# Symmetric sums of keys by VectorE's block turn instead of TensorE, with a new order of the kernel's work

## The chip, the cores and the metric

The kernel runs on one core of a Trainium2 chip. The metric is the device time of one execution in microseconds (us). The core has five engines with instruction queues of their own: TensorE (PE in the profile, its weight loads PEld), VectorE (DVE), ScalarE (ACT), GpSimd (POOL) and SyncE (SP, which here only starts DMAs). They meet through semaphores.

## What is computed

Four batches, four heads, 1088 positions, 32 values per head, in float32. First an attention whose features are products of two sketches of 8 numbers, then a mixing of tokens with phases and a channel step on its output:

```python
a, b = S1 x, S2 x                        # per position: 8 numbers each
phi(x) = a_i * b_j                       # 64 features
kv = sum_s phi(k)_f v_d ;  z = sum_s phi(k)_f
x  = (phi(q) kv) / (phi(q) z + 1e-6)     # attention, heads side by side: B, S, 128
theta = x @ w_theta
y  = w_tok_r @ (x cos theta) + w_tok_i @ (x sin theta)
u  = x + y
out = u + max(u @ w_ch, 0)
```

The denominator phi(q) z can be small, so the kernel computes it with more than float32's precision. It uses that z is S1 K S2 with K the sum of k k^T over positions, a symmetric 32x32 matrix for each head ("key sums"). Each k is split into a rounded part kb (16 bits) and a rest r; K is kb kb^T, exact, plus the rest's terms. With kh = k + kb the term r kh^T, halved and added to its own transpose, gives the rest of K.

## The kernel before

Every operation of the kernel is first recorded with its engine, its buffers and what it depends on, and gets a number. A tuple ORDER, made ahead of time by a planner, then says in which order all operations are issued; each engine works off its own operations in that order, one after another. A second tuple, SLOTS, gives each buffer its place in SBUF or PSUM, and an operation that takes a place over waits for the buffer that was there. So an instruction that waits holds up everything behind it on its engine, and the number of an operation in a list of its engine tells who stands behind whom.

The stages that matter here:

- **key sums** (`key_sums`), one for each batch: TensorE adds up kb kb^T and r kh^T into PSUM. ScalarE copies both out (`ksum`, the second halved). Then `corners`, on TensorE: for each head two matmuls of 32x32 with the identity add the halved rest and its transpose into a third place of the PSUM tile, from which ScalarE later copies it (`e2`).
- **chain** (`chain`), for batch 0, batch 1 and for batches 2 and 3 together: ScalarE rounds K to a level `e0`, VectorE subtracts (`e1`), and `first` multiplies e0, e1 and e2 by the sketch on TensorE. Some ten short steps follow that alternate between VectorE, ScalarE and TensorE and end in the factors of the denominator (`cut`), which the batch's "levels" need.
- **levels, den, num**: the attention's output xT of a batch, with columns of 1152 positions. The queries were rounded before (`q0`) and the rest subtracted by VectorE.
- **turn** (batches 1 to 3): xT is turned to positions by rows, VectorE in 32x32 blocks and then a write to HBM (`far`) and four reads back (`xk`), both issued by SyncE. VectorE multiplies xk by the cosines and sines of theta (`z`).
- **rows**: w_tok has 17 rows of 1088 columns and arrives as 64-bit words, loaded by SyncE into `raw` buffers (class `zs`, 5 places, which z, qt and xk also use). ScalarE makes two conversions of each (L576, L578) and VectorE two integer steps (L316, L312, the custom instruction).
- **mix**: matmuls of z with the rows, in full float32, for batch 0 with all columns of a row at once (three matmuls of 384, 384 and 320 columns), for batch 1 in three groups of columns; batches 2 and 3 together in a Winograd form of seven products. `out` adds x, multiplies by w_ch and stores.

TensorE's mixing matmuls also fill its time between other stages. L332 is the line of the helper for all matmuls, L312 that of tensor-tensor operations on VectorE and GpSimd, L316 and L319 those of other arithmetic; tiles tell them apart.

Of the kernel before, what the change touches and what calls it, by code (L numbers as in the profile page):

```python
# [102 lines left out]
XTURN = (1, 2, 3)  # L103
PARTS = ((0, 384), (384, 544))
# [141 lines left out]
def kernel(  # L246
# [363 lines left out]
    def key_sums(b):  # L610
# [64 lines left out]
        g = kg[b, 0] = buf("g1", (2 if KDMA[b] else 3, D), F32, "ksum")  # L675
        op("A", act(D), lambda: A.copy(g()[:, 0], t()[:, 0]), [(g, 0)], [(t, "s")])
        at("rest", b)
        if KDMA[b]:
            for c in range(NC):
                op("P", TILE32, lambda c=c: heads(1, rc()[:, c * HD:(c + 1) * HD], kh()[:, c]), [(t, "l")], [r, kh])  # L680
            op("A", act(D), lambda: A.mul(g()[:, 1], t()[:, 1], 0.5), [(g, 1)], [t])
            op("P", 0.3, lambda: corners(2, [(g()[:, 1], None), (None, g()[:, 1])]), [t], [(g, 1)])
        else:
            for c in range(NC):
                def two(c=c):
                    x = rc()[:, c * HD:(c + 1) * HD]
                    heads(1, x, kc()[:, c * HD:(c + 1) * HD])
# [791 lines left out]
```

## Time and profile before

| | us |
|---|---|
| median of 3 runs (lowest, highest) | 216.03 (215.62, 216.91) |
| the profiled execution: time | 215.9 |
| its span, first to last instruction | 214.1 |
| TensorE busy in it | 207.0 |
| VectorE busy | 180.7 |
| ScalarE busy | 113.4 |
| GpSimd busy | 37.2 |

The granted TensorE clock was 0.999 over the span. In a timeline row the first number is the start and the second the length in us, then engine, line, operation, tiles written and read, partitions and columns, and the count; in square brackets stands the engine's idle time before it and what ended it. A group row gives the sum in us and, behind the comma, the mean of one in ns. A row of stretches gives the length, then each engine's busy time and count, the clock, the share of the DMA engines and GB/s.

### The profile page before, as it was taken

How to read it: one execution, taken by the hardware profiler on the slowest of the kernel's cores; microseconds unless marked ns; L12 is line 12 of the kernel's file. 1: busy time of each engine (PE TensorE's matmuls, PEld its weight loads, DVE VectorE, ACT ScalarE, POOL GpSimd, SP SyncE). 2: the span in 40 equal slices, each digit the busy share in tenths (PEclk: the TensorE clock that was granted, in tenths of full speed). 3: DMA queues.
4: the chain of work that ended last, by engine and by line, in shares of the span. 5: the costliest groups of instructions: out<-in, count | busy, mean ns of one | idle time of the engine just before them, and what ended most of it. 6: DMA issues, size and time to landing. Idle time of an engine off the chain costs nothing.

```text
span 214.1 us, 5301 instructions
## 1 busy us (share of the span) xinstructions
PE 207.0 (97%) x2140; PEld 149.7 (70%) x2140; DVE 180.7 (84%) x359; ACT 113.4 (53%) x240; POOL 37.2 (17%) x87
## 2 busy tenths in 40 slices
PE   7899999999999999999999999999999999999992
PEld 7677798968867676775665776666676776676682
DVE  1799999999999998997999999988579599995232
ACT  4899999999998986697531333149700000000000
POOL 1272740306400000840003010000040020020002
PEclk9999999999999999999999999999999999999999
DMA  6999999996996994093000443120590011213503
GB/s 222 393 417 418 384 368 418 420 341 120 357 281 214 431 423 201 29 330 72 0 0 7 69 117 106 32 39 22 174 161 0 0 40 27 40 37 52 92 0 67
DMA packets 28780, 37.06 MB, mean 173 GB/s; under 512 B 21332, under 2 KB 23812, under 8 KB 26580
## 3 DMA queue, kind: packets, MB, share of 16 engines
q1 hardware_dynamic: 23268, 31.91, 42.7%
q0 software_dynamic: 1488, 3.15, 7.0%
q10 hardware_dynamic: 4000, 1.67, 3.0%
q8 instruction: 17, 0.28, 0.5%
q14 instruction: 7, 0.06, 0.1%
HBM read 29.84 MB, written 4.00 MB: 158 GB/s over the span
## 4 chain that ended last, share of the span: by engine, by line
PE 55%; DVE 18%; issue 11%; ACT 6%; DMA 6%; POOL 1%; SPq 1%; POOLq 0%; DVEq 0%; ACTq 0%
PE ps L332 49%; DVE big L312 7%; DMA zs<-far 3%; DMA st<-s 2%; PE ps L1053 2%; PE ps L951 2%; ACT big L626 2%; DVE big L319 1%; DMA far<-zs 1%; DVE g L312 1%; DVE zs L312 1%; DVE big L316 1%; ACT g L726 1%; PE ps L361 1%; POOL out L1236 1%
## 5 line engine op out<-in xcount | busy, mean ns | idle before, releaser
L332 PE MATMUL ps<-big,zs 128*128 128x384 f32 (+2 forms) x380 | 108.9, 435 | 0.3 <-DVE zs L312 0.3
L332 PEld LDWEIGHTS ps<-big,zs 128*128 128x128 f32 x380 | 67.1, 190 | 34.8 <-issue 0.9
L1277 ACT COPY g<-ps 80x256 f32<-80x256 f32 x1 | 0.4, 368 | 55.4 <-PE ps L1270 55.4
L332 PE MATMUL ps<-big,big 128*32 128x32 f32 (+2 forms) x352 | 21.8, 234 | 0.0
L312 DVE CUSTOM_DVE_ANT_0 big<-big,big 128x2176 uint16<-128x2176 uint16 x17 | 21.6, 1282 | 0.1
L578 ACT ACTIVATE big<-zs 128x1088 int32<-128x1088 uint32 (+1 forms) x18 | 21.4, 1193 | 0.4 <-DVE g L312 0.4
L576 ACT ACTIVATE big<-zs 128x1088 f32<-128x1088 f32 x17 | 20.8, 1225 | 0.7 <-DVE lv L312 0.5
L332 PEld LDWEIGHTS ps<-big,big 128*32 128x32 f32 (+1 forms) x352 | 14.9, 124 | 5.6 <-issue 1.0
L312 DVE TENSOR_TENSOR big<-big,big 128x544 f32<-128x544 f32 x24 | 16.7, 714 | 0.1
L326 POOL DMA_DIRECT2D g<-big x6 | 5.3, 1071 | 56.2 <-ACT g L1213 56.2
L312 DVE TENSOR_TENSOR zs<-zs,g 128x384 f32<-128x384 f32 (+2 forms) x24 | 9.9, 450 | 4.7 <-DMA zs<-far 4.7
L1236 POOL DMA_DIRECT2D out<-g x6 | 3.8, 633 | 49.7 <-DVE g L1240 31.8
L316 DVE TENSOR_SCALAR big<-big 128x1088 int32<-128x1088 int32 x17 | 12.3, 721 | 0.0
L361 PE MATMUL ps<-idle 128*128 128x112 bf16 (+1 forms) x67 | 10.0, 312 | 1.3 <-POOL idle L363 1.3
L312 DVE TENSOR_TENSOR g<-lv 128x768 f32<-128x768 f32 x12 | 11.2, 950 | 0.1
L312 DVE TENSOR_TENSOR big<-big,hf 128x1152 f32<-128x1152 f32 x8 | 10.7, 1351 | 0.0
L332 PE MATMUL ps<-mf,big 128*128 128x96 f32 (+1 forms) x72 | 10.0, 277 | 0.4 <-DVE big L312 0.4
L332 PE MATMUL ps<-sbk,g 128*128 128x64 f32 x72 | 10.0, 276 | 0.3 <-ACT g L726 0.3
L332 PE MATMUL ps<-w,big 128*128 128x128 f32 (+1 forms) x76 | 10.2, 278 | 0.0
L1139 ACT ACTIVATE g<-g 128x384 f32<-128x384 f32 x12 | 6.3, 531 | 6.9 <-DVE g L319 6.9
L332 PEld LDWEIGHTS ps<-w,big 128*128 128x128 f32 (+1 forms) x76 | 9.4, 189 | 0.5
L332 PEld LDWEIGHTS ps<-sbk,g 128*128 128x128 f32 x72 | 9.0, 191 | 0.8 <-ACT g L726 0.6
(198 smaller groups left out, 352.9 us busy)
## 6 DMA issues: line engine op xcount, KB each, us to landing
zs<-w_tok SPq DMA_DIRECT2D x17, 1088.0 KB, 10.6
big<-k_l SPq DMA_DIRECT2D x5, 576.0 KB, 12.5
big<-v_l SPq DMA_DIRECT2D x4, 576.0 KB, 15.5
big<-q_l SPq DMA_DIRECT2D x3, 576.0 KB, 10.4
big<-hf POOLq DMA_DIRECT2D x3, 576.0 KB, 10.1
far<-zs SPq DMA_DIRECT2D x3, 576.0 KB, 4.4
zs<-far SPq DMA_DIRECT2D x12, 144.0 KB, 4.2
big<-k_l ACTq DMA_DIRECT2D x2, 576.0 KB, 4.4
```

Of the source, the lines that this page charges most:

```text
L312: eng.tensor_tensor(out=o, in0=a, in1=b, op=f)
L316: (eng or V).tensor_scalar(out=o, in0=a, scalar1=s1, scalar2=s2, op0=op0, **kw)
L326: op("G", 0.9, lambda: G.dma_start(dst(), src(), accum_op=ALU.add), w, r, fly=fly)
L332: T.matmul(o, lhs, rhs, start=start, stop=stop, skip_group_check=True)
L361: T.matmul(nowhere()[:, :n], idle()[:, 0:P], idle()[:, :n], start=True, stop=True, skip_group_check=True)
L576: op("A", 0.22 + n * 0.0009, lambda: A.activation(dfn(), words_of(raw(), n)[1].bitcast(F32), AF.Prelu, scale=2.0**-112, alpha=-(2.0**32)), ...
L578: op("A", 0.22 + n * 0.0009, lambda: A.activation(stp(), words_of(raw(), n)[0].bitcast(U32), AF.Copy, scale=2.0**-29), [stp], [raw])
L626: op("A", act(n) + 0.1, lambda: A.activation(flat(r()), kc(), AF.Square, accum_out=km()[:, 1:2]), [r, (km, 1)], [kx])
L951: T.transpose(tr()[:, i * P:(i + 1) * P], x()[:, g * GC + i].rearrange("p h d -> p (h d)"), ident())
L1053: T.transpose(tr()[:, i * P:(i + 1) * P], qp()[:, i * H + 2 * n:i * H + 2 * n + 2].rearrange("p h i j -> p (h i j)"), ident())
L1139: op("A", act(GW), lambda cs=cs: A.activation(cs()[:, 0], cs()[:, 1], AF.Abs), [(cs, 0)], [(cs, 1)])
L1236: E.dma_start(out[b, s0:s0 + n, f * SQ:(f + 1) * SQ].rearrange("(c j) i -> j c i", j=SQ), ot()[f * SQ:(f + 1) * SQ, :n].rearrange("j (c i) ...
```

## The change

For batches 2 and 3 the halved rest is made symmetric without TensorE: VectorE turns the four heads' 32x32 blocks in one instruction (`ksumT`), GpSimd adds the halved rest to it, and in the chain VectorE adds the result to e1. The corner matmuls, the copy e2 and its four matmuls in `first` go. All numbers of operations behind shift by one or two, and ORDER and SLOTS are new.

```diff
+SYM = (2, 3)
...
             op("A", act(D), lambda: A.mul(g()[:, 1], t()[:, 1], 0.5), [(g, 1)], [t])
+            if b in SYM:
+                gt = kk[b] = buf("sm", (D,), F32, "ksumT")
+                vop(D, lambda: V.transpose(out=gt(), in_=g()[:, 1]), [gt], [(g, 1)])
+                op("G", 0.4, lambda: tt(G, gt(), gt(), g()[:, 1], ALU.add), [gt], [(g, 1)], lk=1)
+                return
             op("P", 0.3, lambda: corners(2, [(g()[:, 1], None), (None, g()[:, 1])]), [t], [(g, 1)])
...
             vop(D, lambda g=g, e0=e0, e1=e1: tt(V, e1(), g()[:, 0], e0(), ALU.subtract), [e1], [(g, 0), e0], lk=1)
+            if b in SYM:
+                vop(D, lambda e1=e1, t=t: tt(V, e1(), e1(), t(), ALU.add), [e1], [t], lk=1)
+                continue
+            e2 = gs_[b] = buf("sm", (D,), F32, "e2")
             op("A", act(D), lambda t=t, e2=e2: A.copy(e2(), t()[:, 2]), [e2], [t])
...
-                for h in range(H):
+                for h in range(0 if b in SYM else H):
                     u = slice(h * D, (h + 1) * D)
                     mm(tp()[u, n, 1], gs_[b]()[u], sf()[u, 0:R], False, n == nb - 1)
```

With the renumbering undone, the first 377 entries of ORDER are the same operations as before; on each engine the orders part where the old trace stands at 56 to 66 us. Behind that, row 5's last conversion on ScalarE comes 12 operations later than it did, chain 2 comes ahead of the mixing of row 5, the turn of batch 1 comes 8 operations earlier on VectorE, SyncE issues the loads of rows 12 to 16 behind batch 1's fetch and not ahead of it (row 16's stood between its write and its reads), the mixing of batch 0's rows 10 to 16 stands behind the first rows of batch 1's, and the stores and additions of batches 0 and 1 are spread anew over the Winograd products. The ORDER and SLOTS tuples themselves (some 1000 and 400 numbers) are left out here:

```diff
 ORDER = (
-    0, 1, 29, 32, 4, 2, 5, 3, 34, 30, 356, 50, 33, 102, 44, 96, 6, 108, 103, 36, 7, 51, 366, 54, 144, 8, 97, 10, 9,
...
+    0, 1, 29, 32, 4, 2, 5, 3, 34, 30, 358, 50, 33, 102, 44, 96, 6, 108, 103, 36, 7, 51, 368, 54, 144, 8, 97, 10, 9,
...
```

More of the change, by code (lines that the diff above doesn't have):

```diff
@@ L773, in chain @@
             t, g = kk[b], kg[b, 0]
-            e0, e1, e2 = (buf("sm", (D,), F32, f"e{i}") for i in range(3))
-            es[b], fs[b], gs_[b] = e0, e1, e2
+            e0, e1 = (buf("sm", (D,), F32, f"e{i}") for i in range(2))
+            es[b], fs[b] = e0, e1
             def level(b=b, g=g, e0=e0):
@@ L793, in first @@
                     u = slice(h * D, (h + 1) * D)
-                    mm(tp()[u, n, 1], fs[b]()[u], sf()[u, 0:R], False, False)
-                for h in range(H):
+                    mm(tp()[u, n, 1], fs[b]()[u], sf()[u, 0:R], False, b in SYM and n == nb - 1)
+                for h in range(0 if b in SYM else H):
                     u = slice(h * D, (h + 1) * D)
                     mm(tp()[u, n, 1], gs_[b]()[u], sf()[u, 0:R], False, n == nb - 1)
-        op("P", 0.4 * nb, first, [tp], [x[b] for x in (es, fs, gs_) for b in bs] + [sq, sf])
+        op("P", 0.28 * nb + 0.12 * len(gs_), first, [tp], [x[b] for x in (es, fs, gs_) for b in bs if b in x] + [sq, sf])
         tm = buf("sm", (nb, 2, H, R), F32, "tm")
```

104 rows, old and new, of tables (ORDER, SLOTS) are left out of this document.

## The prediction

> **What bounds the kernel now.** I read the page first, then busy time by stretches, then the waits of TensorE, then its timeline at each place where the change removes something.
>
> ```profile
> span 214.1 us, 5301 instructions
> PE 207.0 (97%) x2140; PEld 149.7 (70%) x2140; DVE 180.7 (84%) x359; ACT 113.4 (53%) x240; POOL 37.2 (17%) x87
> PEclk9999999999999999999999999999999999999999
> ```
> ```profile
> core 0: us, PE busy (x) PEld busy (x) DVE busy (x) ACT busy (x) POOL busy (x), PEclk, DMA share, GB/s
> 57.19:117.60 60.41, 59.75 (x525) 39.81 (x518) 57.40 (x95) 43.87 (x75) 8.27 (x15) 1.00 0.53 184
> 117.60:171.10 53.50, 53.48 (x355) 36.66 (x356) 45.06 (x84) 17.98 (x40) 3.77 (x5) 1.00 0.32 73
> 171.10:209.90 38.80, 38.59 (x170) 27.33 (x170) 27.87 (x57) 0.00 (x0) 3.18 (x5) 1.00 0.24 42
> ```
>
> TensorE is the bound, and at full clock: from 57.19, about where the new order departs from the old one, to 209.90 it is idle for 0.66 + 0.02 + 0.21 = 0.89 us of 152.7. So whatever leaves TensorE's queue comes off the time, and whatever makes TensorE wait is added. VectorE is close behind it in the first stretch, 57.40 of 60.41. The two idle moments worth taking are these:
>
> ```profile
> 100.46 2.74 PE L332 MATMUL ps<-big,zs 128*128 128x320 f32 x8 [0.27 <-DVE zs L312]
> 117.62 1.64 PE L332 MATMUL ps<-mf,big 128*128 128x96 f32 x12 [0.41 <-DVE big L312]
> ```
>
> The first waits for a product of VectorE with batch 1's turned x, and that product waited 1.16 us for the fetch through HBM:
>
> ```profile
> 99.84 1.03 DVE L312 TENSOR_TENSOR zs<-zs,g 128x384 f32<-128x384 f32 x2 [1.16 <-DMA zs<-far]
> ```
>
> The second waits for VectorE's subtraction of batch 3's rounded query, L312.
>
> **TensorE's work that goes.** The corners of batches 3 and 2, and a third of chain 2's first step (TensorE's timeline; start, length, tiles, count):
>
> ```profile
> 67.81 0.26 PE L332 MATMUL ps<-ident,g 32*32 32x32 f32 x8
> 67.90 0.24 PE L332 MATMUL ps<-g,ident 32*32 32x32 f32 x8
> 68.07 0.33 PE L332 MATMUL ps<-big,big 128*32 128x32 f32 x16
> ...
> 77.26 0.26 PE L332 MATMUL ps<-ident,g 32*32 32x32 f32 x8
> ...
> 77.51 0.88 PE L332 MATMUL ps<-g,big 128*32 128x64 f32 x48
> 78.32 0.25 PE L332 MATMUL ps<-sq,sm 32*32 32x16 f32 x8
> 78.41 0.29 PE L332 MATMUL ps<-sf,sm 32*32 32x8 f32 x16
> ...
> 78.84 0.91 PE L332 MATMUL ps<-big,zs 128*128 128x384 f32 x2
> ```
>
> Records of these small matmuls overlap, so the price is read from start to next start, not from lengths: 68.07 - 67.81 = 0.26 and 77.51 - 77.26 = 0.25. Chain 2's first step takes 78.84 - 78.32 = 0.52 for two batches of 8 + 16 records, and half of those with sf go (the e2 part, 8 of 24 per batch): 0.17. Together 0.68 us, 0.3% of the time. Nothing hid it: TensorE has no idle time there, so its next work simply starts sooner.
>
> **What the other engines get.** Per batch, VectorE gets a turn of 128x32 and an addition of 128x32, GpSimd one addition of 128x32, and ScalarE loses one copy.
>
> ```profile
> L1240 DVE STREAM_TRANSPOSE g<-big 128x160 f32<-128x160 f32 x3 | 1.0, 342 | 0.1
> L312 DVE TENSOR_TENSOR sm<-sm,sm 128x32 f32<-128x32 f32 x4 | 0.8, 188 | 0.1
> L312 POOL TENSOR_TENSOR mf<-cf,hm 128x32 f32<-128x32 f32 x2 | 0.4, 229 | 0.0
> L312 POOL TENSOR_TENSOR mv<-s,hm 128x32 f16<-128x32 f32 x2 | 1.6, 830 | 0.0
> L312 DVE TENSOR_TENSOR g<-lv 128x768 f32<-128x768 f32 x12 | 11.2, 950 | 0.1
> ```
>
> The trace has no turn of 32 columns; 160 columns take 0.342, an addition of 32 takes 0.188, and I take 0.21, near the lower row because it has its width. VectorE gets 2 x (0.21 + 0.19) = 0.80 us, 1.06 at most; in the first stretch it has 60.41 - 57.40 = 3.0 idle, 1.16 of it the wait for the fetch, so this fits as a load. ScalarE is idle for 60.41 - 43.87 in that stretch, and its two copies less are worth nothing.
>
> The new wait is on VectorE: its addition of GpSimd's result. For batch 3 five VectorE instructions stand between the turn and the addition, longer than any GpSimd price here. For batch 2 only one does, an outer product of 0.95 (L312, g<-lv). GpSimd's addition costs 0.229 by the one row and 0.830 by the other; 0.23 is hidden, 0.83 plus two hand-offs is not, and what VectorE then loses is 0 to 0.4. Queued behind that addition on VectorE are the second step of row 5 of w_tok, for which TensorE's mixing matmuls of that row wait, and chain 2. [...]
>
> [...]
>
> I take 0.2 for it, the middle of 0 and 0.4, since 0.83 is the row of an instruction with the f16 output and 0.229 the one with this addition's types, and VectorE is busy in this stretch.
>
> **The moves.** VectorE and TensorE, both without slack, meet first where row 5 of w_tok is wanted. VectorE's prices are read from start to start in four consecutive rows, since a record reaches some 0.08 into the next (behind them, two rows of TensorE's timeline and, of its chain of waits, the piece at 76.20):
>
> ```profile
> 60.98 1.28 DVE L312 CUSTOM_DVE_ANT_0 big<-big,big 128x2176 uint16<-128x2176 uint16 x1
> 62.18 0.75 DVE L319 SCALAR_TENSOR_TENSOR big<-lv 128x576 f32<-128x576 f32 x1
> 62.85 0.72 DVE L316 TENSOR_SCALAR big<-big 128x1088 int32<-128x1088 int32 x1
> 63.48 0.45 DVE L312 TENSOR_TENSOR lv<-big 128x288 f32<-128x288 f32 x1
> ...
> 68.50 0.49 PE L332 MATMUL ps<-big,zs 128*128 128x384 f32 x1
> 76.20 0.66 PE ps L1053 x6
> 76.78 0.54 PE L332 MATMUL ps<-g,big 128*32 128x64 f32 x24
> ```
>
> In the new order 24 VectorE operations run from the parting at 56.4 to the end of row 5's second step: two second steps (1.20 each), a first step (0.63), four of 576 columns (0.67), five of 288 (0.4), three of 768 (0.87), ten small ones (2.5 in all): 12.8, so 69.2. TensorE reached the row after the fifth at 68.50; the new order takes the corners from ahead of it (0.26) and puts there a kv sum of batch 2 (77.26 - 76.78 = 0.48), the transposes of num 1 (0.66) and chain 2's first step (0.35): 69.7. So 0.5 to spare, less VectorE's new wait and some hand-offs: TensorE loses 0 to 0.5 here, and I take 0.3, past the middle, because three hand-offs lie in VectorE's 24.
>
> The turn of batch 1 comes 8 places earlier on VectorE, and SyncE's loads of rows 12 to 16 now stand behind its fetch, not before it. Between the turn and the product stand 11 VectorE instructions of 9.2 us (8.4 start to start) and TensorE has 1.1 of other work ahead. Write (median to landing, behind the KB) and fetch:
>
> ```profile
> far<-zs SPq DMA_DIRECT2D x3, 576.0 KB, 4.4
> DMA to landing us min/median/max: 2.6/4.2/5.5
> ```
>
> (the second row: the four parts of the fetch). 4.4 + 4.2 = 8.6 against 9.5: the 0.27 goes. Batch 3's subtraction stands 9 places earlier on VectorE, its first reader on TensorE, levels 3, only 3: the 0.41 goes too, unless ScalarE is late (the rival below).
>
> **Sum** against the profiled execution, 215.9 (span 214.1 and 1.8 around it): -0.68 -0.27 -0.41 +0.2 +0.3 = -0.86, so 215.0; the median of the runs is 216.03, 0.13 above it, so 215.2. Ends: -1.36 without the new waits (214.7) and -0.68 + 0.9 (216.3) with them full and no old wait gone. A measurement of this kernel can tell about 0.5%, 1.08 us, from no change: faster starts below 214.95, slower above 217.1.
>
> **Rivals.** (1) Slower: a row of w_tok lands late and ScalarE's queue stands behind it. Row 11's load uses a raw buffer that row 5 has to leave, and row 5's last conversion on ScalarE is now the 16th operation from 56.6, not the 4th.
>
> ```profile
> 56.61 0.62 ACT L1140 ACTIVATE g<-g,halfpi 128x384 f32<-128x384 f32 x1
> 57.14 0.54 ACT L991 COPY lv<-ps 128x480 f32<-128x480 f32 x1
> 57.58 0.52 ACT L1142 ACTIVATE g<-g 128x384 f32<-128x384 f32 x1
> 58.00 1.21 ACT L578 ACTIVATE big<-zs 128x1088 int32<-128x1088 uint32 x1
> 59.12 0.18 ACT L681 ACTIVATE g<-ps 128x32 f32<-128x32 f32 x1
> ...
> L778 ACT ACTIVATE sm<-g,kg 128x32 f32<-128x32 f32 x4 | 1.3, 324 | 0.0
> DMA to landing us min/median/max: 5.3/10.6/17.8
> 70.50:78.00 7.50, 7.50 (x100) 5.08 (x104) 7.33 (x14) 6.72 (x10) 0.00 (x0) 1.00 1.01 423
> ```
>
> (ScalarE's timeline, a group of level steps, the landing of w_tok's 17 loads, one more stretch.) Again from start to start: ahead of that conversion stand four others (1.15 each), five steps of theta (0.42 to 0.6), four of chain 2's levels (0.32), a copy of 0.44 and three of 0.08: 8.9, and it ends 1.2 later, so the load goes out at 66.7. The conversion that needs it follows after a square of 1152 columns (1.2, by the conversion's 1.21 for 1088), a conversion, six copies of 384 (at most 0.5, by the 0.54 of 480), four more level steps and small ones: 6.5, and about 7.6 with the three results of TensorE that ScalarE waits for (an estimate, a third of a us each). The load alone takes 5.3; with row 10's just ahead, 1088 KB more at 423 GB/s is 2.6, less the 1 us between the issues: 6.9. So 0.7 to spare by this, 3.0 late by the median. Directly behind the waiting conversion stand chain 2's scale (VectorE waits for it) and copies for num 1, whose banks TensorE needs: each us late is a us. At 10.6 it gives 215.2 + 3.0 = 218.2; it decides the sign from a landing of about 8.5 (216.1), and the 0.5% from 9.5. For it: only spare tenths, and rows 12 to 16 then load one after another in the same way, each after a conversion. Against it: the DMA share falls after 57 (0.53), so few loads queue.
>
> [...]
>
> (2) Faster: none of the new waits shows; 216.03 - 1.36 = 214.7. For it: the sums leave room everywhere. Against it: three places have only tenths.
>
> (3) The hand-offs eat what is won: the fetch is waited for as before (0.27 stays) and VectorE's new wait is full: 216.03 - 0.68 - 0.41 + 0.9 = 215.8. This is also the case in which the early fetch does not do what it says.
>
> **Chances.** Forecast 0.33, faster rival 0.24, eaten up 0.13, late rows 0.30. Faster by over 0.5%: 0.26 (rival 2 and the low edge of the forecast); within: 0.44; slower: 0.30. The range leaves out the last of rival 1 and the first of rival 2: 214.4 to 218.2; the forecast's own is 214.7 to 216.3.
>
> **What would show it.** The corner matmuls (ps<-ident,g and ps<-g,ident 32x32) fewer by 32 records, sf rows by 16. TensorE's wait for zs L312 at the first mixing of batch 1 and the wait before levels 3 gone. GpSimd's addition of 128x32 between 229 and 830 ns, VectorE's wait for it under 0.4. TensorE busy at 97% or more of a span near 213.3. Wrong if ScalarE waits over 1 us for w_tok's load, if TensorE idles for more than 0.9 us in all between 57 and the end, or if the first step of chain 2 is no shorter.

## The result: slower by 0.6%, and the profile after

The changed kernel takes 217.29 us in the median (215.89 to 218.86), the kernel before 216.12 beside it: a ratio of 1.0057, 95% interval 1.0036 to 1.0078. The forecast was 215.2, no measurable change and if any a gain; 217.29 lies inside its whole range (214.4 to 218.2) only because rival 1 had widened it; the time moved the other way than the forecast's. (Ratios here and below are of undisturbed runs, so they need not be the quotient of the medians.) The profiled execution after took 217.8 with a span of 216.0, 1.9 more than the one before, so it is one of the slower ones and shows more than the median's loss of 1.2.

The page of the changed kernel, and its busy time by about the same stretches as before:

```profile
span 216.0 us, 5196 instructions
PE 207.8 (96%) x2092; PEld 150.1 (69%) x2092; DVE 181.6 (84%) x363; ACT 113.0 (52%) x238; POOL 37.4 (17%) x89
PEclk9999999999999999999999999999999999999998
```
```profile
57.19:117.60 60.41, 58.29 (x537) 39.91 (x538) 55.77 (x99) 42.00 (x72) 6.65 (x15) 1.00 0.55 183
117.60:171.10 53.50, 53.50 (x342) 36.24 (x341) 48.20 (x87) 19.55 (x41) 6.74 (x8) 1.00 0.32 73
171.10:211.80 40.70, 40.63 (x172) 28.08 (x171) 27.43 (x55) 0.00 (x0) 1.90 (x3) 1.00 0.24 40
```

TensorE has 48 records less and the clock is the same, yet it now idles 60.41 - 58.29 = 2.12 us in the first stretch, where it had 0.66. VectorE has more to do and is busy for less of that stretch (55.77, not 57.40): it waits more too. So the loss is waits, in one stretch. TensorE's table of waits (us in total, times, longest) and the rows of its timeline name them:

```profile
PE ps L362 <- POOL idle L364: 1.3, 1, 1.3
PE ps L333 <- issue: 1.2, 1, 1.2
PE ps L333 <- ACT sm L851: 0.8, 1, 0.8
PE ps L416 <- DVE m L435: 0.5, 1, 0.5
PE ps L333 <- ACT g L677: 0.4, 1, 0.4
PE ps L333 <- DVE hf L317: 0.2, 1, 0.2
```
```profile
57.31 0.70 PE L333 MATMUL ps<-big,big 128*32 128x32 f32 x56 [0.38 <-ACT g L677]
...
67.22 0.33 PE L333 MATMUL ps<-big,big 128*32 128x32 f32 x14
68.73 0.28 PE L333 MATMUL ps<-big,big 128*32 128x32 f32 x10 [1.18 <-issue]
...
71.63 0.25 PE L333 MATMUL ps<-sq,sm 32*32 32x16 f32 x8
71.71 0.22 PE L333 MATMUL ps<-sf,sm 32*32 32x8 f32 x8
...
71.99 0.59 PE L333 MATMUL ps<-big,zs 128*128 128x384 f32 x1
...
78.97 0.87 PE L333 MATMUL ps<-g,sm 128*64 128x384 f32 x4 [0.82 <-ACT sm L851]
```

What the forecast took away is away: no wait for VectorE's product (zs) or subtraction (big) is left in the table, and chain 2's first step takes 71.99 - 71.63 = 0.36, where it took 0.52. The wait of 1.3 is at the very start, in both kernels. Three waits are new, 2.38 us together (2.12 of it inside the stretch, since most of the 0.38 lies just ahead of 57.19): 0.38 for ScalarE's copy of batch 3's key sums, in the middle of that batch's rest; 1.18 in the middle of batch 2's rest, with 14 of its matmuls done and 10 to go, in which TensorE waited for nothing that the profile knows ("issue"); 0.82 for chain 2's scale (L851).

Behind the last stands the queue of ScalarE, behind VectorE's turn (L685) the same queue a little earlier; the POOL rows are GpSimd's two additions:

```profile
64.41 2.35 ACT L579 ACTIVATE big<-zs 128x1088 int32<-128x1088 uint32 x2 [2.44 <-DMA zs<-w_tok]
66.64 1.21 ACT L577 ACTIVATE big<-zs 128x1088 f32<-128x1088 f32 x1
67.73 1.19 ACT L579 ACTIVATE big<-zs 128x1088 int32<-128x1088 uint32 x1
69.08 0.20 ACT L682 ACTIVATE g<-ps 128x32 f32<-128x32 f32 x1 [0.15 <-PE ps L333]
...
77.66 1.20 ACT L579 ACTIVATE big<-zs 128x1088 int32<-128x1088 uint32 x1 [1.52 <-DMA zs<-w_tok]
78.76 0.16 ACT L851 ACTIVATE sm<-ps 128x8 f32<-128x8 f32 x1
```
```profile
67.33 0.29 DVE L313 TENSOR_TENSOR sm<-ps,sm 128x128 f32<-128x128 f32 x1 [1.04 <-PE ps L916]
...
69.30 0.21 DVE L685 STREAM_TRANSPOSE sm<-g 128x32 f32<-128x32 f32 x1 [1.32 <-ACT g L682]
69.44 0.92 DVE L313 TENSOR_TENSOR g<-lv 128x768 f32<-128x768 f32 x1
70.50 0.19 DVE L313 TENSOR_TENSOR sm<-sm,sm 128x32 f32<-128x32 f32 x1
70.61 1.28 DVE L313 CUSTOM_DVE_ANT_0 big<-big,big 128x2176 uint16<-128x2176 uint16 x1
```
```profile
63.36 0.37 POOL L313 TENSOR_TENSOR sm<-sm,g 128x32 f32<-128x32 f32 x1 [6.95 <-DVE sm L685]
69.59 0.88 POOL L313 TENSOR_TENSOR sm<-sm,g 128x32 f32<-128x32 f32 x1 [5.87 <-DVE sm L685]
```

Row 9's conversion (64.41) waits 2.44 for its load; behind it stand the two of row 6, that of row 5 (67.73 to 68.92), and batch 2's halving (69.08), for which the turn waits. Only when row 5 is converted does row 11's load go out (68.94); its conversion (77.66) waits 1.52, and chain 2's scale follows it. In the kernel before, the conversions of rows 5 and 6 stood ahead of row 9's; ScalarE came to it only at 64.55 and did not wait:

```profile
64.55 1.24 ACT L578 ACTIVATE big<-zs 128x1088 int32<-128x1088 uint32 x1
```

### The profile page after: what moved, and what is told of

It reads as the page before. It is cut to its first block, busy times and chain, and to the rows that moved or that the text cites. A ratio compares the mean times of both kernels' runs of the same rounds, so it can differ in the third digit from the quotient of the medians.

```text
span 216.0 us, 5196 instructions
## 1 busy us (share of the span) xinstructions
PE 207.8 (96%) x2092; PEld 150.1 (69%) x2092; DVE 181.6 (84%) x363; ACT 113.0 (52%) x238; POOL 37.4 (17%) x89
## 4 chain that ended last, share of the span: by engine, by line
PE 78%; DMA 6%; issue 6%; ACT 5%; DVE 2%; POOL 1%; POOLq 0%; SPq 0%; ACTq 0%
PE ps L333 72%; DMA zs<-w_tok 4%; DMA st<-s 2%; PE ps L362 2%; PE ps L961 2%; PE ps L729 2%; ACT big L579 1%; POOL out L1246 1%; PE ps L1063 1%; ACT g L1146 1%; DVE g L1250 1%; DVE big L320 1%; ACT lv L1001 1%; ACT big L577 1%; DVE hf L317 0%
## 5 line engine op out<-in xcount | busy, mean ns | idle before, releaser
L333 PE MATMUL ps<-big,big 128*32 128x32 f32 (+2 forms) x352 | 22.3, 235 | 1.6 <-issue 1.2
L1001 ACT COPY lv<-ps 128x480 f32<-128x480 f32 x12 | 6.6, 562 | 6.4 <-PE ps L333 6.3
L320 DVE SCALAR_TENSOR_TENSOR big<-ps,even,big 128x160 f32<-128x160 f32 (+1 forms) x10 | 4.7, 494 | 6.1 <-PE ps L333 6.1
```

Source lines behind the costliest of these rows:

```text
L320: (eng or V).scalar_tensor_tensor(out=o, in0=a, scalar=s, in1=b, op0=op0, op1=op1)
L333: T.matmul(o, lhs, rhs, start=start, stop=stop, skip_group_check=True)
L1001: op("A", act(480), lambda g=g, lp=lp: A.copy(lv().rearrange("p l (c n) -> p l c n", n=HR)[:, :, g * GC:(g + 1) * GC], lp().rearrange("p c ...
```

## The experiments

Every kernel computes the whole reference. Each is set against the kernel before, run beside it on the same chip:

| run | kernel | median us | ratio, 95% interval |
|---|---|---|---|
| 1 | symmetric sums, old order | 215.90 | 1.0007 [0.9982, 1.0033] |
| 2 | corners, new order | 218.03 | 1.0099 [1.0073, 1.0125] |
| 3 | changed, row 11 behind | 217.57 | 1.0074 [1.0052, 1.0096] |
| 4 | 3 and key sums' copy behind | 217.49 | 1.0059 [1.0035, 1.0083] |
| 5 | four moves | 216.72 | 0.9992 [0.9965, 1.0019] |
| 6 | changed, rest's wait later | 217.59 | 1.0024 [0.9999, 1.0050] |
| 7 | as 1, addition earlier | 216.60 | 0.9993 [0.9970, 1.0016] |
| 8 | before, rest's wait earlier | 216.63 | 0.9984 [0.9961, 1.0008] |
| 9 | 5 and halving first | 216.11 | 0.9964 [0.9934, 0.9994] |
| 10 | before, two waits | 217.19 (one run) | |
| 11 | changed, one wait | 219.41 (one run) | |
| 12 | as 9, with corners | 216.99 | 1.0023 [1.0005, 1.0042] |
| 13 | 5 and row 9 behind | 214.89 | 0.9955 [0.9934, 0.9976] |
| 14 | changed, two moves | 215.26 | 0.9963 [0.9945, 0.9982] |
| 15 | as 13, with corners | 217.41 | 1.0063 [1.0033, 1.0092] |

The diffs are pieces of ORDER. In the new numbering the turns are 239 (batch 2) and 294 (batch 3), GpSimd's additions 240 and 295, VectorE's 303 and 306.

### The sums or the order (runs 1, 7, 2)

Run 1, the old order in the new numbering:

```diff
-293, 236
+294, 295, 236
...
-303, 399
+305, 306, 239, 240, 401
...
-239, 300, 400, 202, 301, 208
+302, 402, 202, 303, 208
```

> The symmetric sums by VectorE and GpSimd, but the old ORDER: each new operation stands where the corners and the copies e2 stood (batch 3's turn where its corners were, batch 2's turn and addition well ahead of chain 2's first step). Theory A (leaving TensorE out of the key sums is worth what its start-to-start prices say, and what was lost in the changed kernel is lost by its order): TensorE has 0.5 to 0.7 us less to do and nothing else moves, so 215.4 to 215.7 where the kernel before has 216.1, a ratio of 0.997 to 0.998; the two waits for VectorE (0.27 at the first mixing of batch 1, 0.41 before levels 3) stay. Rival B (the hand-offs turn, GpSimd addition, VectorE addition cost what TensorE saves, in any order): 216.1 or more, with TensorE waiting at chain 2's first step or VectorE over 0.5 us for GpSimd.

Run 7, in that order:

```diff
-302, 402, 202, 303, 208
+302, 303, 402, 202, 208
```

> The symmetric sums in the old ORDER again, with VectorE's addition of batch 2's result moved up by one place, ahead of the second step of row 9 (1.28 us), behind which it made TensorE wait 0.35 at chain 2's first step. Theory A: that wait goes and the saving on TensorE shows in full: 215.4 to 215.6, ratio 0.997 to 0.998. Rival B: VectorE, not TensorE, sets the pace there and the time stays within 0.1 of the kernel before.

Run 2, the new order in the old numbering (corners 239, 293; copies e2 301, 304):

```diff
-294, 295
+293, 304
...
-239, 403, 240
+239, 301, 401
```

> The new ORDER, but corners and e2 on TensorE and ScalarE as before, each where the turn stands in the new order. Theory A: the order alone loses about 1.7 us, so 217.6 to 218.1 (the changed kernel's 217.3 plus the 0.5 to 0.7 of TensorE's work that comes back), ratio 1.007 to 1.009. Rival B: the order is neutral and the symmetric sums cost the 1.2 us, then 216.1. In the profile theory A wants the three losses of the changed kernel again: TensorE waiting 0.4 for ScalarE's copy of key sums near 57, 0.8 for chain 2's scale near 78; the pause of 1.2 near 67 in which TensorE waits for nothing that shows will be there if it belongs to the order, and not if it is chance of one execution.

Of TensorE's rows with a wait, those that the reading rests on, in run 1, in run 7, and in run 2, here with a row of ScalarE:

```profile
78.50 0.24 PE L333 MATMUL ps<-sf,sm 32*32 32x8 f32 x8 [0.35 <-DVE sm L313]
```
```profile
78.75 2.10 PE L333 MATMUL ps<-big,zs 128*128 128x384 f32 x6 [0.36 <-DVE big L313]
...
100.81 3.39 PE L333 MATMUL ps<-big,zs 128*128 128x320 f32 x10 [0.70 <-DVE zs L313]
```
```profile
70.81 0.26 PE L333 MATMUL ps<-ident,g 32*32 32x32 f32 x8 [0.95 <-ACT g L682]
...
76.19 0.55 PE L1063 MATMUL ps<-ident,g 128*128 128x128 f32 x3 [0.56 <-ACT g L1067]
...
66.08 0.19 ACT L793 COPY sm<-ps 128x32 f32<-128x32 f32 x1 [4.14 <-PE ps L333]
```

The order loses, and the sums do not: with them the old order is at 1.0007, without them the new order is at 1.0099. But run 2's loss is not the changed kernel's. Of the three waits that theory A wanted, only the one near 57 is there (0.40); the pause and the wait for chain 2's scale are not, and 0.95 and 0.56 are new. They come with the place that was given to the corners: the copy e2 of batch 3 (L793) stands behind them in ScalarE's queue and waits 4.14 us for them, to 66.08, and batch 2's halving, for which batch 2's corners wait, stands behind that copy. So the number that theory A named came by another way, and the step from 1.0099 to 1.0057, about 0.9 us, is not the worth of the sums alone. In the old order the sums are worth nothing that these runs can tell. Moving the addition took its wait of 0.35 away and put one of 0.36 for row 9's second step on the mixing right behind, as in rival B of run 7. That VectorE's added work takes back what TensorE saves fits this, but how much of it is not shown: run 7's interval also holds 0.997 to 0.998, theory A's ratio.

### The two waits for ScalarE (runs 3, 4)

Run 3 moves row 11's conversion (410) behind chain 2's scale (314) and a copy (577); run 4 also the copy of batch 3's key sums (283) behind that batch's rest (285 to 292):

```diff
-311, 410, 312, 576, 313, 314, 569, 577, 562
+311, 312, 576, 313, 314, 569, 577, 410, 562
...
-540, 283, 227, 228, 286, 287, 288, 289, 290, 291, 292, 495, 377, 547, 498
+540, 227, 228, 286, 287, 288, 289, 290, 291, 292, 495, 377, 547, 498, 283
```

> The changed kernel with one move: ScalarE's first conversion of row 11, which waits for that row's load, goes two places back, behind chain 2's scale and the last copy of num 1, group 2. Theory A (rival 1 of the prediction is at work: the late load holds up chain 2's scale, and TensorE waits 0.8 us for the bank): the wait of 0.82 near 78 goes, nothing takes its place, 216.4 to 216.7, ratio 1.002 to 1.003. Rival B: row 11 is then late for its own mixing or the next bank is as late, and the time stays at 217.2 to 217.4. Rival C: the wait near 78 came from the pause near 67 in the profiled execution, and is not there in others: then this move is worth nothing.

> The changed kernel with that move and a second one: ScalarE's copy of batch 3's key sums is issued after the rest of batch 3 on TensorE, not in the middle of it, where TensorE waited 0.38 us for it near 57.3 in the changed kernel. Theory A: both waits go, 0.8 + 0.4: 216.0 to 216.3, ratio 0.999 to 1.001, so what is left of the loss is the pause near 67. Rival B: ScalarE's later copy makes chain 2 later by as much: as with the first move alone.

Each wait that was aimed at went, and the time stayed: 1.0074 and 1.0059 beside 1.0057. In run 4 TensorE then waits at levels 2, for a subtraction that VectorE has behind batch 1's turn, which waits for ScalarE again, and the pause is there too:

```profile
68.06 0.32 PE L333 MATMUL ps<-big,big 128*32 128x32 f32 x11 [1.05 <-issue]
...
83.07 0.96 PE L333 MATMUL ps<-mf,big 128*128 128x96 f32 x6 [0.49 <-DVE big L313]
```

The gains of 0.8 and 1.2 us that were expected did not come: a wait at the end of a chain of late work, once removed, shows the next one (run 3's profile has waits of 0.34, 0.24 and 0.59 instead, beside a pause of 0.25).

### The pause (runs 6, 8, 10, 11)

The page's DMA part has a queue "instruction" (q8), with packets of 16 KB. The one at issue ran between 62.5 and 65.2 in the kernel before and between 65.2 and 67.5 in the changed one (windows of the DMA view, packets, MB, share):

```profile
q8 instruction: 1, 0.02, 2.8%
```
```profile
q8 instruction: 1, 0.02, 3.1%
```

Their starts are 63.5 and 66.2. In runs 3 and 4 it began at 65.5, in 1 and 2 at 63.0 and 62.9. Where it was late, TensorE stopped at the same place of its stream (busy time up to the pause; the changed kernel, run 3):

```profile
0.00:68.70 68.70, 64.98 (x1234) 52.34 (x1235) 59.01 (x145) 60.02 (x142) 21.86 (x63) 1.00 0.90 323
```
```profile
0.00:67.85 67.85, 64.41 (x1234) 51.99 (x1235) 58.78 (x145) 58.88 (x141) 21.82 (x63) 1.00 0.92 327
```

1234 matmuls both times (1233 in run 4); with weight loads and TensorE's own records of waits counted in, it is 2497 records in these and in runs 4 and 10. From 1.3 to 1.5 us after the packet's end TensorE went on (67.35 to 68.73 in the changed kernel). Run 6 moves three sums ahead of batch 2's rest (229 to 237), whose first matmul waits for GpSimd's additive DMA; run 8 moves work of the kernel before (493) so that this matmul stands right behind the mixing, as in the changed kernel:

```diff
-400, 229, 230, 385, 231, 555, 232, 233, 234, 263, 196, 384, 189, 190, 235
+400, 263, 196, 189, 229, 230, 385, 231, 555, 232, 233, 234, 384, 190, 235
```
```diff
-379, 493, 550, 229
+379, 550, 229
...
-237, 189, 426
+237, 189, 493, 426
```

> The changed kernel with the last of those moves alone (kv sums and the chain-1 sum ahead of batch 2's rest). Theory A: the instruction transfer begins at about 63 and the pause of 1.2 near 67 is gone; batch 2's rest ends as before or sooner, so nothing is later; 216.0 to 216.5, ratio 1.000 to 1.002. Rival B: transfer at 65.5 or later and a pause at the 2497th record as before, 217.3.

> The kernel before, with one move on TensorE: three transposes (theta 0, group 2) go from ahead of batch 2's rest to behind it, so that the matmul that waits for GpSimd's additive transfer stands right behind the mixing, as in the changed kernel. Theory A: the instruction transfer near 63.5 now begins at 65.5 or later, and TensorE pauses at the 2497th record: 0.3 to 1.0 us, 216.4 to 217.1, ratio 1.0015 to 1.005. Rival B: transfer near 63.5 as before, no pause, 216.1.

In run 6 the transfer began at 63.7 and the pause was gone. But in run 8 theory A missed: the transfer began at 62.9, and there is no pause. The place alone does not make it. What differs is the form of the wait. In the changed kernel ScalarE's copy of batch 2's key sums (228) is issued ahead of the rest, and the first matmul has two things to wait for; the trace has a record of a wait alone in TensorE's queue there, at 64.71, the moment at which the additive DMA landed (issued at 54.12, 10.6 to landing). The kernel before has no such record between 57.00 and 68.22. Run 10 gives the kernel before such a wait, run 11 takes it from the changed kernel:

```diff
-505, 549, 282, 398
+505, 549, 282, 228, 398
...
-499, 238, 228, 302
+499, 238, 302
```
```diff
-283, 227, 228, 286
+283, 227, 286
...
-237, 556
+237, 228, 301, 302, 556
```

> The kernel before, with two moves: the three transposes of theta 0, group 2, behind batch 2's rest (as tried alone, without effect), and ScalarE's copy of batch 2's key sums ahead of that rest in the order of issue. The first matmul of the rest then has two things to wait for, that copy and GpSimd's additive transfer, and the second wait becomes an instruction of its own in TensorE's queue, as it is in the changed kernel. Theory A (an instruction of its own that waits keeps TensorE's queue from reading on, and so from asking for its next instructions, until the transfer has landed; a wait carried by the matmul itself does not): the instruction transfer begins at 65.3 to 66.3, not at 63, and TensorE pauses at the 2497th record for 0.2 to 1.0 us. Rival B (the late instruction transfer is not made by that wait): it begins at about 63, no pause.

> The changed kernel, with ScalarE's copy of batch 2's key sums (and the level of chain 2 and VectorE's subtraction that need it) issued behind batch 2's rest. The rest's first matmul is at its old place right behind the mixing, and still waits for GpSimd's additive transfer, but that wait now stands in the matmul itself, not in an instruction of its own. Theory A: the instruction transfer begins at about 63 and the pause at the 2497th record is gone; chain 2 starts up to 1 us later. Rival B (the place behind the mixing makes it): transfer at 65.5 or later, pause as before.

Run 10, TensorE's timeline, and the DMA view of its window 65.2 to 67.5 (start 65.8):

```profile
68.42 0.26 PE L332 MATMUL ps<-big,big 128*32 128x32 f32 x4 [0.36 <-issue]
```
```profile
q8 instruction: 1, 0.02, 3.4%
```

Theory A held both ways, in one profile each: a pause behind the 1234th matmul, in a kernel that had none; and in run 11 the transfer at 62.8 and no pause. (Run 11 takes longer because it makes chain 2's level late, and TensorE waits 2.41 near 70.) The four pauses lasted 0.25, 0.36, 1.05 and 1.18 us.

The other profiles limit this. In run 2 the copy is issued first as well, but the corners of batch 3 stand ahead of the rest; there is no such record near 64, and no late transfer. In runs 5, 9 and 13 there is one, at 65.6, but their transfers had begun before it (63.2 to 64.1), and there is no pause. This fits a wait that does harm only where it stands ahead of the place in the queue at which the transfer is asked for; where that place is, no run shows.

Run 6 also shows why the pause alone gives back only part: 1.0024 (a gain of 0.7 us, whose interval overlaps that of the changed kernel). With TensorE on time it waits for VectorE, and VectorE for ScalarE (timeline of run 6, TensorE, then VectorE, then ScalarE):

```profile
70.49 0.84 PE L1063 MATMUL ps<-ident,g 128*128 128x128 f32 x6 [0.89 <-DVE g L313]
71.94 2.10 PE L333 MATMUL ps<-big,zs 128*128 128x384 f32 x6 [0.24 <-DVE big L313]
...
79.09 0.87 PE L333 MATMUL ps<-g,sm 128*64 128x384 f32 x4 [0.98 <-ACT sm L851]
...
69.29 0.21 DVE L685 STREAM_TRANSPOSE sm<-g 128x32 f32<-128x32 f32 x1 [1.78 <-ACT g L682]
...
64.66 2.33 ACT L579 ACTIVATE big<-zs 128x1088 int32<-128x1088 uint32 x2 [2.74 <-DMA zs<-w_tok]
```

### ScalarE's queue (runs 5, 9, 13, 14)

Run 5 has the moves of runs 4 and 6 and VectorE's subtraction (348) ahead of batch 1's turn; run 9 also the halving (238) ahead of row 5's conversion (380):

```diff
-315, 563
+315, 348, 563
...
-235, 236, 380, 237, 556, 507, 238
+235, 236, 237, 238, 380, 556, 507
```

> The changed kernel with four moves: the two of the run before (row 11's first conversion behind chain 2's scale; batch 3's copy of key sums behind its rest), VectorE's subtraction of batch 2's rounded query ahead of batch 1's turn (levels 2 waited 0.5 to 0.6 for it near 83 once the wait near 78 was gone), and on TensorE the kv sums of batches 3 and 2 and the chain-1 sum ahead of batch 2's rest, not inside it. The last is aimed at the pause: in three executions of the new order TensorE stood still at the same record (matmuls and weight loads counted together, the 2497th), 1.3 to 1.5 us after one 16 KB instruction transfer that began at 65.5 to 66.2; in the three executions without a pause that transfer began at 62.9 to 63.5. In the new order the first matmul of batch 2's rest, which waits for GpSimd's additive transfer (landing 64.4 to 64.7), is the next thing behind the mixing; in the others some 13 records or more stand between. Theory A (TensorE's queue asks for its next instructions only once it gets past that waiting matmul): transfer at about 63, no pause, all waits gone, 215.2 to 215.8, ratio 0.996 to 0.999. Rival B (that transfer comes when it likes): a pause of up to 1.2 stays, 216.4 or more.

> The run with four moves, and a fifth: batch 2's rest is issued, and ScalarE's halving of it follows, ahead of ScalarE's conversion of row 5 (1.2 us), not behind it. With the pause gone, VectorE stood 1.6 us idle at batch 2's turn, waiting for that halving, and the outer product of num 1 queued behind the turn made TensorE wait 0.65, row 5's second step 0.24. Theory A (the turn put a new wait for ScalarE into VectorE's queue, and VectorE hands it on to TensorE): both waits go, 0.6 to 0.9 less than the run with four moves, a ratio of 0.994 to 0.997 to the kernel before. Rival B: row 5 comes 0.2 later and VectorE is full anyway, so TensorE waits as long at the next place: ratio as with four moves, 0.998 to 1.000.

Run 5 brings the loss back (0.9992), though not by the way expected, for TensorE still waits 0.65 and 0.24 near 70. Run 9 has the ratio that its theory A named, but in its profile the turn waited longer than ever, so its mechanism failed (timeline of ScalarE, VectorE, TensorE):

```profile
65.83 2.31 ACT L579 ACTIVATE big<-zs 128x1088 int32<-128x1088 uint32 x2 [4.12 <-DMA zs<-w_tok]
...
69.34 0.21 DVE L685 STREAM_TRANSPOSE sm<-g 128x32 f32<-128x32 f32 x1 [2.42 <-ACT g L682]
...
70.54 0.85 PE L1063 MATMUL ps<-ident,g 128*128 128x128 f32 x6 [1.43 <-DVE g L313]
```

So it is not the 1.2 us of one conversion: it is row 9's load, which lands 1.7 to 4.1 us after ScalarE has come to it (in the changed kernel and in runs 3, 4, 5, 6, 9 and 11). Run 13 moves row 9's conversion (400) in run 5 behind row 5's; run 14 does only this and run 6's move to the changed kernel:

```diff
-306, 400, 263
+306, 263
...
-236, 380, 237
+236, 380, 400, 237
```

> The run with four moves, and ScalarE's first conversion of row 9 behind the conversions of rows 6 and 5 instead of ahead of them (row 9 is wanted some 20 us later; the fifth move of the earlier run is not in it). Theory A (ScalarE's wait for row 9's load holds up batch 2's halving, that VectorE's turn, that the outer product of num 1 behind it, and that TensorE): ScalarE converts rows 6 and 5 while row 9 is under way, the halving comes at about 67, VectorE's wait at the turn falls from 1.6 to under 0.6, TensorE's 0.65 and 0.24 near 70 go; row 11's load, which follows row 5's conversion, goes out 3 us sooner. 214.9 to 215.4, ratio 0.992 to 0.996. Rival B: the halving is early but VectorE is full, so TensorE waits a little further on: 0.997 to 1.000.

> The changed kernel with only two moves: kv sums and the chain-1 sum ahead of batch 2's rest on TensorE (no pause), and row 9's first conversion behind those of rows 6 and 5 on ScalarE. Row 11's conversion is at its old place, but its load now goes out 3 us sooner. Theory A: pause, turn and row 11 were what was lost, so all of it comes back but the 0.4 near 57: 215.4 to 216.0, ratio 0.995 to 0.998. Rival B: one of them alone is not enough, as the pause alone was not (1.0024): 1.001 or more, with TensorE waiting 0.6 or more near 70 or 78.

Run 14: the first stretch, and in the timeline VectorE's turn and ScalarE's conversions of rows 5 and 9 (63.88) and 11 (74.59):

```profile
57.19:117.60 60.41, 60.41 (x545) 41.55 (x546) 57.97 (x103) 43.91 (x71) 8.58 (x15) 1.00 0.55 185
```
```profile
67.69 0.21 DVE L685 STREAM_TRANSPOSE sm<-g 128x32 f32<-128x32 f32 x1 [0.33 <-ACT g L682]
...
63.88 2.32 ACT L579 ACTIVATE big<-zs 128x1088 int32<-128x1088 uint32 x2
...
74.59 1.24 ACT L579 ACTIVATE big<-zs 128x1088 int32<-128x1088 uint32 x1
```

TensorE has no idle time in the stretch, ScalarE waits for no load there, and row 11 is 3 us earlier. Two moves turn 1.0057 into 0.9963 (215.26 us, 215.12 to 215.47 over its runs). Run 13 has the lowest median here, but its interval and run 14's overlap. Row 9's move without the one against the pause was not run.

### Corners in the mended orders (runs 12, 15)

The orders of runs 9 and 13 with the pieces of run 2's diff.

> The order with five moves, but with corners and e2 on TensorE and ScalarE, each corner group where the turn stood. Theory A (with the order mended, the symmetric sums are worth TensorE's 0.5 to 0.7 us): a ratio 0.002 to 0.003 above that of the run with five moves. Rival B (VectorE is the other bound there, and what it gets costs as much as TensorE saves): within 0.001 of it, or below.

> The order of the run with four moves and row 9 behind, with corners and e2 on TensorE and ScalarE where the turn stood, so without the symmetric sums on VectorE. Theory A (in an order without those waits the symmetric sums are worth TensorE's 0.5 to 0.7 us): a ratio 0.002 to 0.004 above the run it is made from. Rival B (VectorE gives back what TensorE saves, as it seems to in the old order): within 0.001 of it.

1.0023 beside 0.9964 and 1.0063 beside 0.9955, 1.3 and 2.3 us: more than TensorE's 0.7, so neither theory has the size. In run 15 the corners stand where the turn stood and TensorE itself waits for the halving, 0.94, and 0.55 for a copy behind it. As in run 2, the copy e2 of batch 3 holds ScalarE's queue, here for 3.60 us to 65.71 (3.95 to 66.13 in run 12), ahead of the conversions and the halving that run 13 had brought forward. So these two runs do not have the mended queue of ScalarE that they were meant to have, and they do not price the sums. Only the old order was made for corners, and there the sums are worth nothing that can be told; what they are worth in a good new order stays open.

## Why the prediction was wrong

**The terms that were right.** Corners and first step: 0.68 forecast; 48 records less and 0.36 for 0.52 measured. The waits of 0.27 and 0.41: gone, in every profile of the new order (in those of the old one the first was 0 to 1.49). The turn: 0.21 forecast, 0.21 measured. VectorE's wait for GpSimd's addition: 0.2 forecast; the outer product ended at 70.36 and the addition began at 70.50, so 0.14. Run 14, which has all of this and the new waits mended but for 0.38, is 0.8 us faster than before (0.9963). That the sum was -0.86 does not prove it to a tenth, for run 14 has another order than the one that was summed up.

**The step that failed** is the sum's term for new waits, +0.2 for VectorE's wait and +0.3 for row 5: 0.5, and both at the hand-over of row 5 from VectorE to TensorE. In the changed kernel's profile TensorE's new waits are 2.38 (1.18, 0.82, 0.38), and none of them is there. The sum has no term for ScalarE: its waits for loads were left to rival 1, and the pause and the copy of key sums were put at nothing. Runs 6 and 14 show what this missed: with the pause mended the ratio is 1.0024, with row 9's conversion moved back as well it is 0.9963. Two of the prediction's own signs of being wrong are in the profile: ScalarE waits 2.44 and 1.52 for loads of w_tok, and TensorE idles for 2.19 us between 57.19 and 211.80, where 0.9 was the limit.

**The working of the 0.3** was wrong too: "69.2" by durations and three hand-offs. Row 5's second step began at 70.61 and ended at 71.89, 2.7 later. Of that, 1.32 is the turn's wait: the sum of 24 operations took the turn as a load of 0.21 and never asked what it waits for, which is ScalarE's halving, behind row 9's conversion, which waits for its load. The prediction named the new wait for GpSimd behind the turn and not the one ahead of it. Another 1.04 is VectorE's wait for a transposition on TensorE (L916), and 0.14 the one for GpSimd. In the changed kernel's profile the pause hid this lateness from TensorE; run 6 shows its price, 0.89 + 0.24.

**Rival 1 came true, with its cause further up the queue.** Its mechanism and its place (row 11, chain 2's scale behind it) were right, with a chance of 0.30. Its working put row 5's conversion by a sum of ScalarE's durations, and so row 11's load at 66.7 and a landing of 6.9; the conversion ended at 68.92, 2.2 later by row 9's wait of 2.44, and the load took 8.7. TensorE lost 0.82 (0.98 in run 6). The sum of ScalarE's queue held only rows 11 to 16 to be at risk, though row 9's load stands in the same queue ahead of all that was summed.

**Two waits were in nobody's account**: 0.38 for the copy of key sums, which the order of issue put between matmuls of the rest; and the pause, 0.25 to 1.18. The account of the two profiles does not close: 2.38 of new waits less the 1.36 that went is 1.0 of the 1.9 us between them, and 0.2 is there already at the start, ahead of the change. The rest, some 0.7, is not traced.

**GpSimd, loads and transfers of instructions.** All 22 of GpSimd's additions in 11 profiles ended 0.10 to 0.12 us after the VectorE instruction that was running when they began, whether they took 0.37, 0.57, 0.87 or 1.13 us (the two POOL rows above: 63.73 and 70.47, VectorE's instructions 63.62 and 70.36; in run 1 68.87 and 71.61, VectorE's 68.76 and 71.51). In two of the 22 (0.57) that VectorE instruction has a single tensor input. What held the addition until then, no run shows. VectorE lost 0.14 and not 0.4: the addition ended 0.11 behind one outer product of 0.92.

Row 10's load took 4.8 from issue to landing, and row 11's, issued 1.05 behind it, 8.7; the prediction's 5.3 for a load alone, the least of the 17 before, was near the first and far from the second.

The instruction queue moved 16 packets of 16 KB for the changed kernel's 4231 records on TensorE and 17 for 4329 in the kernel before, one for about every 260 records, and the four pauses came behind the same record. That these packets are TensorE's instructions is my reading of that count and that place; no row names the engine. In the changed kernel TensorE's queue was held at a wait of its own until 64.71, some 220 records of small matmuls followed within 2 us (65.73 to 67.55), and the transfer, from 66.21 to 67.35, ended 1.4 before TensorE went on. In run 12 TensorE has one more wait of the kind "issue", 0.20 at 60.48, in the mixing; what made it is not traced.

## What to carry to other kernels

When an operation moves to another engine, ask first what its input waits for in the queue that makes it, and carry every transfer in that queue as a landing time with a spread, not as a duration. A conversion that waits for a load should not stand ahead of work that is wanted sooner; one such move, with one that mended TensorE's instruction stream, was worth 2 us here, and the runs' spread went from 3.0 us to 0.4 (1.3 in run 13). When a removed wait doesn't pay, look for the next wait in the same chain before giving up the theory: runs 3, 4 and 6 each took a real wait away and gained 0.7 us at most.

## What the hardware showed that I had not expected

TensorE stood still in four profiles, for want of instructions as I read them: where a record in its queue that is only a wait stood until 64.4 to 64.7, the next 16 KB came 1.4 to 3.4 us later than in the other profiles (65.5 to 66.2, not 62.8 to 64.1), and after some 220 records of small matmuls TensorE stopped, for 0.25 to 1.18 us; it went on 1.3 to 1.5 us after the transfer's end. The same dependence without such a record did not do this (runs 8 and 11: transfers at 62.9 and 62.8, no pause). Issuing an unrelated copy ahead of a matmul, on the same PSUM tile, was enough to change the form of the wait (run 10 beside run 8: transfer at 65.8 and at 62.9).
